# A Fourier convolution with expert routing on one core: the first phase's stores and positions change queues, and its reload comes in three parts

## The chip, the cores and the metric

The kernel runs on one core of one Trainium2 chip. The metric is device time in microseconds (us). Timed runs were made without a profile; one more execution was recorded by the hardware profiler, and every row of a profile below comes from that one.

## The reference

Two computations follow one another. The first is a long causal convolution by Fourier transforms with a filter made by a small network; its product with x is the input of a mixture of experts.

```python
h_mlp = np.maximum(pos_emb @ w1, 0.0) @ w2
h_filt = h_mlp * np.exp(-0.01 * pos)[:, None]
u = x * v                                    # (4, 11456, 128)
y = irfft(rfft(u, n=2S, axis=1) * rfft(h_filt, n=2S, axis=0), n=2S, axis=1)[:, :S]
x = (x * y).reshape(B * S, D)
...
out[do_compute] = xc + gate_w * (relu(xc @ w1[e]) @ w2[e])   # the best expert of each token
```

Rows of the product whose score against w_skip isn't positive are passed through; each other row goes to its best expert of eight. All of it is in float32.

## The kernel before, in words

The transform of length 3840 (three blocks of the sequence) is done in two stages, of 60 and of 64 points. The program has three parts, one after the other: first_phase makes the first stage, freq_phase the second stage, the product with the filter and the first stage back, and out_phase the last stage back, the routing and the experts.

**first_phase** interleaves two generators on the same engines. `First.data(step, pool)` handles one of 16 steps for the first quarter of the features. A step loads a block of x and v of 768 KB (`load`, L178, tile xv), multiplies the two (`mult`, L185), and runs two half steps: each does two matmuls with the 60-point table (L202) into PSUM and two copies by ScalarE into a staging tile (L204). A step's result, 120 rows of 1536 floats, is stored to DRAM as x1d (`store`, L190). All of xv, us (the product) and xs (staging) lie in a tile named wf in the profile; there are 3, 2 and 4 buffers of them. `First.filt` makes the filter's side. It first runs 12 pieces: positions of 256 KB are loaded (`positions`, L232, tile post, 4 buffers, issued 3 pieces ahead), multiplied with w1 (L240) and put through a relu by ScalarE (L241, tile h). Then, for 8 chunks with 3 blocks each, it makes small matmuls with w2 (L267), multiplies by the window on VectorE (L268), does the 60-point stage (L248), and ScalarE copies into fx (L250, 2 buffers each for two halves). After the third block of a chunk the two halves of fx, 120 rows each, are stored as x1f (L256). `first_phase` advances the filter's generator by some two yields for each half step, so that both end together.

Loads run up to three steps ahead (`ahead`). A store of x1d is put off: `data` appends it to a list at the end of its step, and `store` issues it after the first half of the next step, or at once after the last step of a quarter.

**Queues.** Each engine issues its DMAs in its own program order, and a DMA that has to wait holds up what is queued behind it on that engine. Before the change SyncE issues the loads of xv and all stores of x1d, alternating; GpSimd issues the positions and the stores of x1f; ScalarE issues four small loads at the start. In the queue lists of the profile SP is SyncE.

**freq_phase** runs 60 iterations, 15 for each quarter of the features. `load(n)` (L359 to L363) brings the tables c2 (first quarter only), a slice of x1d (128 rows, 4 by 384 floats) and of x1f into the tile x, up to three iterations ahead, in 4 buffers. An iteration does the 64-point stage on TensorE (L373, tile xp), the products with the filter on VectorE (L385, L393), sums on GpSimd (L465, L466), the stage back on TensorE (L404), copies by ScalarE (L405), and a store of z (L414, zd). In the first three quarters it also runs the first stage of the next quarter: `others` calls `mult`, `ahead` and `data` with SyncE's queue for its stores. Six half steps of that (LEAD, three steps) run before the first iteration, on loads that the first phase has issued; the later products run on GpSimd.

The first iteration can only start when its x has landed, which needs x1d of all 16 steps and all of x1f.

Of the kernel before, what the change touches and what calls it, by code (L numbers as in the profile page):

```python
# [22 lines left out]
K1, N2 = 60, 64  # L23
# [5 lines left out]
DH = D // NP  # L29
W = D + 1  # L30
# [113 lines left out]
class First:  # L144
# [3 lines left out]
    Q = 2  # L148
# [3 lines left out]
    XV, US, XS = 3, 2, 4  # L152
# [17 lines left out]
    def ahead(self, step):  # L170

        while self.loaded < min(step + self.XV, self.ALL):
            self.load(self.loaded)
            self.loaded += 1
# [11 lines left out]

    def store(self):

        for dst, xs in self.late:
            self.nc.sync.dma_start(dst, xs)  # L190
        self.late = []

    def data(self, step, pool):
        nc, Q, RUN = self.nc, self.Q, self.RUN
# [3 lines left out]
        for q in range(Q):  # L198
# [6 lines left out]
            if q == 0:  # L205
                self.store()
            if q < Q - 1:
                yield
        self.late.append((self.x1d[h][:, :, 2 * Q * ch:2 * Q * (ch + 1)].rearrange("k c m w -> (k c) m w"), xs))
        if ch == self.STEPS - 1:  # L210
            self.store()
        yield

    def filt(self, fc, fp, pool):


        nc, i = self.nc, self.i
# [11 lines left out]
        def positions(blk, k):  # L229

            pt = fp.tile([128, P], F32, name="post", bufs=4)
            nc.gpsimd.dma_start(pt, i["post"][blk, k // P])  # L232
            return pt
        posts = [positions(*pc) for pc in pieces[:3]]
        yield
        for n, (blk, k) in enumerate(pieces):
            if n + 3 < len(pieces):
                posts.append(positions(*pieces[n + 3]))
            ps = pool.tile([128, P], F32, name="fa")
            nc.tensor.matmul(ps, w1, posts.pop(0), start=True, stop=True)  # L240
            nc.scalar.activation(hs[blk][:, k:k + P], ps, AF.Relu)  # L241
            yield

        def forward(ch, blk, hw, xs):
# [9 lines left out]
            for p in range(2):  # L254
                n0 = p * H2 + ch * M
                nc.gpsimd.dma_start(self.x1f[:, :, n0:n0 + M].rearrange("k c m w -> (k c) (m w)"),  # L256
                                    xs[p].rearrange("k m h s d -> k (m h s d)"))
# [18 lines left out]
def first_phase(tc, fi):  # L276

    with (
# [8 lines left out]
        pace = (pieces - FLEAD) / (fi.Q * (fi.STEPS - FEND))  # L287
        next(f)
# [18 lines left out]
def freq_phase(tc, nc, i, fi, zd, c3, spare, loads):  # L307
# [9 lines left out]
    with (  # L317
# [35 lines left out]
        def load(n):  # L353
# [8 lines left out]
            nc.sync.dma_start(x1[:, :, 0:fi.RUN], fi.x1d[h][ks].rearrange("k c n w -> (c n) k w"))  # L362
            nc.sync.dma_start(x1[:, :, fi.RUN:], fi.x1f[ks, :, :, h * w:(h + 1) * w].rearrange("k c n w -> (c n) k w"))  # L363
            return x1
# [995 lines left out]
```

## Time and profile before

| | us |
|---|---|
| median of 3 runs | 1625.7 (1624.03 to 1628.4) |
| the profiled execution | 1626.78 |
| its span on the core | 1625.0 |
| TensorE (PE) busy | 1537.8 |
| VectorE (DVE) busy | 1203.4 |
| GpSimd (POOL) busy | 1084.8 |
| ScalarE (ACT) busy | 794.3 |
| first L373, where the second stage starts | 142.78 |

The median is 1.1 us below the profiled execution, and the span 1.8 us below it. Times in rows count from the span's start. In rows of the timeline the columns are start, duration, engine, line, operation, tiles and count, and in brackets the idle time before and what ended it; SPq, ACTq and so on are the engines' instruction queues. The list by windows gives for each stretch its length, then busy time and number of instructions of PE, PEld (weight loads), DVE, ACT and POOL, then the granted TensorE clock, the DMA engines' mean busy share and the GB/s moved; the share adds up the time of packets, and can pass 1. A row of waits names who waited, for what, us in total, how often, and the longest.

### The profile page before, as it was taken

How to read it: one execution, taken by the hardware profiler on the slowest of the kernel's cores; microseconds unless marked ns; L12 is line 12 of the kernel's file. 1: busy time of each engine (PE TensorE's matmuls, PEld its weight loads, DVE VectorE, ACT ScalarE, POOL GpSimd, SP SyncE). 2: the span in 40 equal slices, each digit the busy share in tenths (PEclk: the TensorE clock that was granted, in tenths of full speed). 3: DMA queues.
4: the chain of work that ended last, by engine and by line, in shares of the span. 5: the costliest groups of instructions: out<-in, count | busy, mean ns of one | idle time of the engine just before them, and what ended most of it. 6: DMA issues, size and time to landing. Idle time of an engine off the chain costs nothing.

```text
span 1625.0 us, 26505 instructions
## 1 busy us (share of the span) xinstructions
PE 1537.8 (95%) x8272; PEld 961.0 (59%) x8272; DVE 1203.4 (74%) x2424; ACT 794.3 (49%) x1677; POOL 1084.8 (67%) x850
## 2 busy tenths in 40 slices
PE   7985999999999999996789999999989999999997
PEld 2552444444444444442347766666767888888997
DVE  1324877888788799993877777777887777777886
ACT  4552455444544544442235544544345655556774
POOL 1112988888888878870156647855677888867885
PEclk9996999999999999997889999999999999999999
DMA  7998999999999799968978768877631111111110
GB/s 283 333 339 315 379 377 377 356 329 335 321 343 338 255 265 316 312 160 295 301 222 255 229 214 257 255 223 240 209 87 33 47 45 47 45 37 37 38 36 23
DMA packets 198532, 361.92 MB, mean 223 GB/s; under 512 B 64650, under 2 KB 138778, under 8 KB 198350
## 3 DMA queue, kind: packets, MB, share of 16 engines
q1 hardware_dynamic: 181078, 320.12, 58.9%
q0 software_dynamic: 16704, 38.89, 8.5%
q8 instruction: 67, 1.10, 0.3%
q10 hardware_dynamic: 608, 1.20, 0.2%
q14 instruction: 75, 0.61, 0.1%
HBM read 216.96 MB, written 145.69 MB: 223 GB/s over the span
## 4 chain that ended last, share of the span: by engine, by line
PE 84%; DMA 6%; DVE 5%; issue 3%; POOL 1%; ACT 1%; SPq 0%; DVEq 0%; ACTq 0%; POOLq 0%
PE ps L404 20%; PE xp L373 12%; PE bank L782 6%; PE y L1018 5%; PE ps L202 5%; PE my L834 4%; PE my L832 4%; PE hp L700 4%; PE my L833 4%; PE hp L702 4%; PE hp L701 4%; PE mh L700 2%; PE tp L1031 2%; PE mh L702 1%; PE mh L701 1%
## 5 line engine op out<-in xcount | busy, mean ns | idle before, releaser
L404 PE MATMUL ps<-y,c 128*128 128x512 f32 x720 | 331.3, 597 | 0.3
L465 POOL TENSOR_TENSOR y<-y,p 128x2048 f32<-128x2048 f32 x59 | 267.7, 4537 | 68.8 <-DVE p L393 68.8
L706 POOL DMA_INDIRECT out<-o,ids x186 | 199.9, 1075 | 123.3 <-DVE o L713 87.0
L404 PEld LDWEIGHTS ps<-y,c 128*128 128x128 f32 x720 | 133.4, 190 | 173.0 <-issue 155.9
L637 POOL DMA_INDIRECT xt<-out,ids x186 | 193.1, 1038 | 49.3 <-issue 30.6
L393 DVE TENSOR_TENSOR p<-xp,g 128x1024 f32<-128x1024 f32 x240 | 217.4, 947 | 0.0
L393 DVE TENSOR_TENSOR y<-xp,g 128x1536 f32<-128x1536 f32 x120 | 210.8, 1757 | 4.1
L821 DVE SCALAR_TENSOR_TENSOR hh<-hp,hh 128x1024 fp32r<-128x1024 f32 x130 | 158.4, 1219 | 68.3 <-ACT hh L820 68.1
L405 ACT COPY z<-ps 128x512 f32<-128x512 f32 x180 | 105.6, 586 | 176.5 <-PE ps L404 167.5
L820 ACT ACTIVATE hh<-hp 128x1024 fp32r<-128x1024 f32 x130 | 134.2, 1032 | 75.4 <-PE hp L702 75.4
L589 POOL DMA_INDIRECT lists<-pl,lies x32 | 53.6, 1676 | 141.0 <-DVE step L1116 72.3
L466 POOL TENSOR_TENSOR y<-y,p 128x1024 f32<-128x1024 f32 x59 | 139.0, 2356 | 4.6
L677 DVE TENSOR_TENSOR ws<-wf,ws 128x1024 fp32r<-128x1024 f32 x104 | 126.7, 1219 | 15.5 <-ACT ws L672 12.1
L610 POOL MEMSET idle<- 128x512 f16 x248 | 134.6, 543 | 0.2
L1018 PE MATMUL y<-zt,c 128*64 128x512 f32 x384 | 114.1, 653 | 19.8 <-DMA zt<-zd 11.2
L700 PE MATMUL hp<-hl,ws 128*128 128x512 f32 (+1 forms) x344 | 123.3, 359 | 3.5 <-DVE tb L626 1.9
L202 PE MATMUL ps<-wf,c 60*120 60x384 f32 x512 | 111.8, 532 | 14.8 <-DVE wf L185 14.3
L782 PEld LDWEIGHTS bank<-wd,h 128*128 128x128 f32 x896 | 104.2, 191 | 31.5 <-issue 31.4
L373 PE MATMUL xp<-x,wf 128*128 128x480 f32 x256 | 115.5, 575 | 7.3 <-issue 3.6
L204 ACT COPY wf<-ps 120x384 f32<-120x384 f32 x256 | 105.5, 493 | 29.5 <-PE ps L202 28.9
L702 PE MATMUL hp<-hl,ws 128*128 128x512 f32 (+1 forms) x344 | 116.4, 338 | 0.0
L834 PE MATMUL my<-hh,ws 128*128 128x512 f32 (+1 forms) x344 | 116.3, 338 | 0.0
(162 smaller groups left out, 3062.1 us busy)
## 6 DMA issues: line engine op xcount, KB each, us to landing
wf<-xv SPq DMA_DIRECT2D x64, 768.0 KB
zt<-zd SPq DMA_DIRECT2D x64, 768.0 KB
x1d<-wf SPq DMA_DIRECT2D x64, 720.0 KB
x<-x1d SPq DMA_DIRECT2D x60, 768.0 KB
zd<-z SPq DMA_DIRECT2D x118, 384.0 KB
out<-xm SPq DMA_DIRECT2D x96, 258.0 KB
ox<-xo SPq DMA_DIRECT2D x96, 256.0 KB
x1f<-fx POOLq DMA_DIRECT2D x16, 720.0 KB
```

The lines of the kernel that those rows point to most:

```text
L202: nc.tensor.matmul(ps[p], self.c1[rows], u[rows, q * RUN:(q + 1) * RUN], start=True, stop=True)
L373: nc.tensor.matmul(xp[:, k, 0:(NS + NB) * DH], c2(n % PER * KS + j * KH + k), x1[:, j * KH + k], start=True, stop=True)
L393: nc.vector.tensor_tensor(o[:, :, :, j * KH:(j + 1) * KH].rearrange("p s a k b d -> p (s a) k b d"), x[:, None].broadcast_to([128, m, KH, ...
L404: nc.tensor.matmul(zps, c3[:, a, :], y[:, blk, a], start=(a == 0), stop=(a == 1))
L465: nc.gpsimd.tensor_tensor(y[:, 1:], y[:, 1:], p1, ALU.add)
L637: ins = nc.gpsimd.indirect_dma_start(out=xt[:, j], out_offset=None, in_=self.rows[0:have], in_offset=bass.IndirectOffsetOnAxis(ap=ids[:, j ...
L700: nc.tensor.matmul(hp, w[:, 0, c], hl[:, 0], start=True, stop=False)
L702: nc.tensor.matmul(hp, w[:, 1, c], hl[:, 0], start=False, stop=True)
L706: ins = nc.gpsimd.indirect_dma_start(out=self.rows, out_offset=bass.IndirectOffsetOnAxis(ap=ids[:, j:j + 1], axis=0), in_=o, in_offset=Non ...
L782: nc.tensor.matmul(bank[:, j * D:(j + 1) * D], h[f][:, j * 128:(j + 1) * 128], wd[s][:, f * D:(f + 1) * D], start=(f == 0), stop=(f == F / ...
L834: nc.tensor.matmul(y, w2[:, 1, c], h[:, 0], start=False, stop=(f == F // 128 - 1))
L1018: nc.tensor.matmul(y[p * 64:(p + 1) * 64], c4s[ch // C4][:, ch % C4, p, :], z[:, NP * p:NP * (p + 1)], start=True, stop=True)
```

## The change

In the first phase four things are moved, and one in the second:

- Stores of x1d of the first quarter are issued by ScalarE right behind the copies that fill their staging tile, at the end of their own step. Of the 120 rows ScalarE's queue takes 112 (EVEN) and GpSimd's the last 8. Stores of the later quarters stay whole on SyncE's queue, but also at the end of their own step.
- Each store of x1f becomes two, of 112 and 8 rows, both from GpSimd.
- Positions are loaded by SyncE, four pieces ahead and not three: two before the first load of xv, two behind it, and each later one behind the matmul that frees its buffer.
- In the first iteration's reload, x1d comes in two parts around x1f: positions 0 to 47 of the 64 in each half of the rows (steps 0 to 11), then x1f, then the last 16. These are five DMAs in place of two.

The diff, cut to its core:

```diff
@@ -27,6 +27,7 @@
 N = L * NS
 NP = 4
 DH = D // NP
+EVEN = 2 * K1 // 16 * 16
 W = D + 1
 T = 256
 
@@ -167,9 +168,9 @@
         nc.sync.dma_start(self.c1, i["c1"])
         self.loaded, self.late = 0, []
 
-    def ahead(self, step):
-
-        while self.loaded < min(step + self.XV, self.ALL):
+    def ahead(self, step, most=XV):
+
+        while self.loaded < min(step + most, self.ALL):
             self.load(self.loaded)
             self.loaded += 1
 
@@ -184,10 +185,18 @@
             eng = self.nc.vector if step < self.STEPS + LEAD // self.Q else self.nc.gpsimd
             eng.tensor_tensor(self.us[step % self.US][rows], xv[:, 0], xv[:, 1], ALU.mult)
 
+    def shares(self, eng):
+
+        nc = self.nc
+        if eng is nc.sync:
+            return [(slice(0, 2 * K1), eng)]
+        return [(slice(0, EVEN), eng), (slice(EVEN, 2 * K1), nc.gpsimd)]
+
     def store(self):
 
-        for dst, xs in self.late:
-            self.nc.sync.dma_start(dst, xs)
+        for dst, xs, eng in self.late:
+            for rows, by in self.shares(eng):
+                by.dma_start(dst[rows], xs[rows])
         self.late = []
 
     def data(self, step, pool):
@@ -202,13 +211,10 @@
                 nc.tensor.matmul(ps[p], self.c1[rows], u[rows, q * RUN:(q + 1) * RUN], start=True, stop=True)
             for p in range(2):
                 nc.scalar.copy(xs[:, 2 * q + p], ps[p])
-            if q == 0:
-                self.store()
             if q < Q - 1:
                 yield
-        self.late.append((self.x1d[h][:, :, 2 * Q * ch:2 * Q * (ch + 1)].rearrange("k c m w -> (k c) m w"), xs))
-        if ch == self.STEPS - 1:
-            self.store()
+        self.late.append((self.x1d[h][:, :, 2 * Q * ch:2 * Q * (ch + 1)].rearrange("k c m w -> (k c) m w"), xs, nc.sync if h else nc.scalar))
+        self.store()
         yield
 
     def filt(self, fc, fp, pool):
@@ -229,15 +235,17 @@
         def positions(blk, k):
 
             pt = fp.tile([128, P], F32, name="post", bufs=4)
-            nc.gpsimd.dma_start(pt, i["post"][blk, k // P])
+            nc.sync.dma_start(pt, i["post"][blk, k // P])
             return pt
-        posts = [positions(*pc) for pc in pieces[:3]]
+        posts = [positions(*pc) for pc in pieces[:2]]
+        yield
+        posts += [positions(*pc) for pc in pieces[2:4]]
         yield
         for n, (blk, k) in enumerate(pieces):
-            if n + 3 < len(pieces):
-                posts.append(positions(*pieces[n + 3]))
             ps = pool.tile([128, P], F32, name="fa")
             nc.tensor.matmul(ps, w1, posts.pop(0), start=True, stop=True)
+            if n + 4 < len(pieces):
+                posts.append(positions(*pieces[n + 4]))
             nc.scalar.activation(hs[blk][:, k:k + P], ps, AF.Relu)
             yield
 
@@ -253,8 +261,10 @@
                 return
             for p in range(2):
                 n0 = p * H2 + ch * M
-                nc.gpsimd.dma_start(self.x1f[:, :, n0:n0 + M].rearrange("k c m w -> (k c) (m w)"),
-                                    xs[p].rearrange("k m h s d -> k (m h s d)"))
+                there = self.x1f[:, :, n0:n0 + M].rearrange("k c m w -> (k c) (m w)")
+                here = xs[p].rearrange("k m h s d -> k (m h s d)")
+                for rows in (slice(0, EVEN), slice(EVEN, 2 * K1)):
+                    nc.gpsimd.dma_start(there[rows], here[rows])
         last = iter(())
         for ch in range(H2 // M):
             xs = [fp.tile([2 * K1, M, NP, NB, DH], F32, name=f"fx{p}") for p in range(2)]
@@ -285,6 +295,8 @@
         left = 0.0
         pieces = NB * 64 * H2 // 512 + 2 * NB * H2 // 4
         pace = (pieces - FLEAD) / (fi.Q * (fi.STEPS - FEND))
+        next(f)
+        fi.ahead(0, 1)
         next(f)
         fi.ahead(0)
         fi.mult(0)
@@ -359,8 +371,16 @@
                 nc.sync.dma_start(c2(ks.start, KS), i["c2"][k])
             x1 = qx.tile([128, KS, (NS + NB) * DH], F32, name="x1")
             w = NB * DH
-            nc.sync.dma_start(x1[:, :, 0:fi.RUN], fi.x1d[h][ks].rearrange("k c n w -> (c n) k w"))
+            def rows(lo, hi):
+                for c in range(2):
+                    nc.sync.dma_start(x1[c * N2 + lo:c * N2 + hi, :, 0:fi.RUN], fi.x1d[h][ks, c, lo:hi].rearrange("k n w -> n k w"))
+            if n == 0:
+                rows(0, N2 - 16)
+            else:
+                nc.sync.dma_start(x1[:, :, 0:fi.RUN], fi.x1d[h][ks].rearrange("k c n w -> (c n) k w"))
             nc.sync.dma_start(x1[:, :, fi.RUN:], fi.x1f[ks, :, :, h * w:(h + 1) * w].rearrange("k c n w -> (c n) k w"))
+            if n == 0:
+                rows(N2 - 16, N2)
             return x1
 
         def spread(n, j):
```

## The prediction

> **What bounds the kernel now.** I read the chain of waits first, to see which stretches aren't TensorE work. Its answer over the whole span names the longest pieces in order of time; these are the ones around the end of the first phase, and two from behind it.
>
> ```profile
> 17.23 8.31 DMA post<-post
> ...
> 118.83 18.50 DMA x1d<-wf
> 138.06 4.58 DMA x<-x1f
> 142.78 5.36 PE xp L373 x8
> 166.58 3.43 PE ps L404 x8
> 176.68 3.43 PE ps L404 x8
> ```
>
> From 142.78 us on the chain is TensorE, with one piece of L404 every 10.10 us (176.68 - 166.58). Ahead of that stand DMA landings: a block of positions early on, then the last store of x1d, which takes 18.50 us, then the reload. So whatever makes the first xp (L373) start earlier moves all that follows by the same amount, as long as the second stage keeps its 10.10 us. The question is thus what sets 142.78.
>
> Next I asked for engine busy times by window. In each row the last two columns are the DMA engines' mean busy share and the GB/s moved.
>
> ```profile
> 0.00:30.00 30.00, 18.92 (x38) 6.15 (x40) 3.83 (x4) 10.63 (x19) 6.88 (x16) 0.90 0.91 335
> 30.00:45.00 15.00, 15.00 (x120) 8.72 (x118) 4.87 (x7) 8.79 (x19) 0.74 (x2) 0.98 0.60 167
> 45.00:130.00 85.00, 70.78 (x488) 40.85 (x484) 23.73 (x32) 42.49 (x92) 7.61 (x15) 0.92 0.96 339
> 60.00:110.00 50.00, 46.77 (x341) 27.58 (x340) 16.05 (x21) 24.74 (x54) 5.18 (x10) 0.97 0.96 337
> 130.00:142.70 12.70, 5.83 (x16) 2.42 (x16) 1.66 (x2) 3.44 (x8) 0.00 (x0) 0.50 0.59 198
> 160.00:250.00 90.00, 89.92 (x254) 39.19 (x253) 72.58 (x89) 45.17 (x118) 81.54 (x30) 1.00 1.02 378
> ```
>
> The first phase is bound by transfers: from 45 to 130 us the share stands at 0.96, though not at the 1.02 of the second stage. It has a hole at 30 to 45 us (0.60, 167 GB/s) and another after 130 us (0.59, 198 GB/s). The waits of 45 to 130 us agree: engines wait for landings of loads and of stores, and SyncE's queue stands 52.5 us at the x1d stores for ScalarE's copies.
>
> ```profile
> DVE wf L185 <- DMA wf<-xv: 21.9, 6, 8.3
> ACT fx L250 <- DMA x1f<-fx: 11.9, 5, 2.8
> ```
> ```profile
> SPq L190 <- ACT wf L204: 52.5, 11, 8.3
> ```
>
> **Part one: 112 and 8 rows.** The transfers of the phase, from the page's list of issues and the list for 0 to 150 us:
>
> ```profile
> wf<-xv SPq DMA_DIRECT2D x64, 768.0 KB
> x1d<-wf SPq DMA_DIRECT2D x64, 720.0 KB
> ...
> x1f<-fx POOLq DMA_DIRECT2D x16, 720.0 KB
> ```
> ```profile
> post<-post POOLq DMA_DIRECT2D x12, 256.0 KB
> ```
>
> A quarter of the 64 belongs to the first phase: 16 loads of 768 KB against 16 and 16 stores of 720 KB, so 35% of these bytes are loads (128 rows) and 65% stores (120 rows). Suppose a store of 120 rows uses 15 of the 16 DMA engines, 8 rows each. Then each of the 15 carries 0.35/16 + 0.65/15 = 0.0652 of the bytes and the sixteenth 0.0219; if the 15 never rest, the mean share is (15 + 0.0219/0.0652)/16 = 0.958. The rows show 0.96. With 112 rows (7 to each engine) and the last 8 spread over further engines, each carries 0.0625, which is 4.1% less. From 45 us to the last landing (118.83 + 18.50 = 137.33) that is 92 x 0.041 = **3.8 us**. The Trainium skill has the same rule ("DMA: Bandwidth & Descriptors", section "Why a DMA increments its semaphore by 16 and not by 1": a transfer runs on the largest number of engines up to 16 that divides its rows, so 15, 16 and 8 here); no row of this trace shows a transfer of 8 rows.
>
> The bounds: nothing if the sixteenth isn't the reason, and 9.5 us if the stretch then reaches the second stage's 378 GB/s (92 x (1 - 339/378)). I take 3.8, since the share in the row is the one that 15 engines give.
>
> The price is issues. GpSimd gets 16 x 8-row issues and 16 more for x1f, SyncE loses 16 and ScalarE gains 16.
>
> ```profile
> L256 POOL DMA_DIRECT2D x1f<-fx x15 | 7.8, 525 | 62.3 <-ACT fx L250 62.3
> ```
> ```profile
> L190 SPq DMA_DIRECT2D x1d<-wf x21: 348/349/2376, 16.8 to 169.6; - x21
> ```
>
> GpSimd: 32 x 0.525 = 17 us, hidden, as it is idle 62.3 us in that stretch alone. It now stands in order at x1d rows and x1f rows, both released by ScalarE's copies in the order of its queue. ScalarE: 16 x 0.35 = 5.6 us, or 16 x 2.38 = 38 us if each issue is as slow as the slowest. Its room is 50 - 24.74 = 25 us of every 50, so about 50 us in 100: both ends are hidden on average, and I take nothing. Queued behind a slow issue are the copies that free TensorE's accumulators.
>
> **Part two: the opening.** Before, SyncE's queue alternates loads and stores:
>
> ```order
> L178 DMA wf<-xv 128x1536 x4
> L359 DMA wf<-c 128x512
> L190 DMA x1d<-wf 120x1536
> L178 DMA wf<-xv 128x1536
> L190 DMA x1d<-wf 120x1536
> L178 DMA wf<-xv 128x1536
> ```
>
> After the change the same place holds loads and positions (post):
>
> ```order
> L238 DMA post<-post 128x512 x2
> L179 DMA wf<-xv 128x1536
> L238 DMA post<-post 128x512 x2
> L179 DMA wf<-xv 128x1536 x2
> L238 DMA post<-post 128x512 x2
> L179 DMA wf<-xv 128x1536
> L238 DMA post<-post 128x512 x4
> L179 DMA wf<-xv 128x1536
> ```
>
> The first two positions now lead the loads, four are ahead, not three, and no store stands in front of a load. On ScalarE's queue the stores follow the step's own copies:
>
> ```order
> L249 ACTIVATE h_76<-fa 128x512 x2
> L213 COPY wf<-ps 120x384 x2
> L199 DMA x1d<-wf 112x1536
> L249 ACTIVATE h_77<-fa 128x512 x2
> L213 COPY wf<-ps 120x384 x2
> ```
>
> What that does to the hole is read from the timeline of before:
>
> ```profile
> 21.99 0.96 DVE L185 TENSOR_TENSOR wf<-wf 124x768 f32<-124x768 f32 x1 [5.08 <-PE ps L202]
> 25.68 3.75 PE L240 MATMUL fa<-post,fw 128*128 128x512 f32 x4 [3.76 <-DMA post<-post]
> 33.52 2.31 PE L267 MATMUL fa<-fw,h 128*64 128x128 f32 x32
> 34.51 0.35 SPq L190 DMA_DIRECT2D x1d<-wf  x1
> 34.95 0.33 SPq L178 DMA_DIRECT2D wf<-xv  x1
> ```
>
> TensorE stands 3.76 us for a position that took 8.31 us to land; step 2 is late for it, so its store is issued at 34.51, and behind it in the queue a load at 34.95 whose buffer the product of 21.99 freed at 22.95. Meanwhile the DMA engines ran dry. After the change that load waits only for the product, and goes about 12 us earlier. The hole lacks (339 - 167) x 15 us = 2.58 MB against the stretch behind it; at 339/0.96 = 353 GB/s that is 7.3 us. The bounds are nothing and 7.3; I take **6.0**, nearer to the full size, since loads, positions and stores no longer block one another, but the positions now share a queue with loads of 768 KB (2.2 us each at 353).
>
> **Part three: the end of the phase.** Before, the reload of the first x (786 kB from x1d, then x1f) follows all stores. After the change SyncE's queue reads:
>
> ```order
> L179 DMA wf<-xv 128x1536 x10
> L376 DMA x_882<-x1d 48x4x384 x2
> L179 DMA wf<-xv 128x1536 x2
> L381 DMA x_882<-x1f 128x4x96
> L376 DMA x_882<-x1d 16x4x384 x2
> ```
>
> Three quarters of the rows come from steps 0 to 11 and load early; two lead loads stand behind them.
>
> ```profile
> 113.94 3.19 ACT L204 COPY wf<-ps 120x384 f32<-120x384 f32 x8
> 116.84 1.91 SPq L178 DMA_DIRECT2D wf<-xv  x1
> 118.83 1.98 SPq L190 DMA_DIRECT2D x1d<-wf  x1
> 135.61 0.96 DVE L185 TENSOR_TENSOR wf<-wf 124x768 f32<-124x768 f32 x1 [4.90 <-DMA wf<-xv]
> 136.71 2.92 PE L202 MATMUL ps<-wf,c 60*120 60x384 f32 x8 [2.94 <-DVE wf L185]
> ```
>
> The early part is 0.75 x 786 = 590 kB, which costs 590/353 = 1.7 us within the bound stretch. The tail, 137.33 to 142.65 (138.06 + 4.58), is 5.3 us; without those bytes ahead of it, about 4.58 - 1.7 + 1.1 for three issues = 4.0. Net: **-0.4 us** (a loss). The last store is issued at the end of its copies, 117.13, not at 118.83 behind a load: **1.7 us** (from nothing, if the bytes alone count, to 4.4 us, the two lead loads that no longer stand ahead of it). What is late next is the last lead load: from the product at 135.61 to the end of L202 at 139.63 are 4.0 us, as long as the new tail, so TensorE isn't held longer by it.
>
> **Part four: the lead stores and the second stage.** There a store of x1d stays on SyncE, but now follows its own step, not the one before.
>
> ```profile
> 165.06 0.38 SPq L362 DMA_DIRECT2D x<-x1d  x1
> ...
> 181.25 0.42 SPq L190 DMA_DIRECT2D x1d<-wf  x1
> 181.78 1.24 SPq L414 DMA_DIRECT2D zd<-z  x2
> ```
> ```profile
> 182.59 1.63 ACT L204 COPY wf<-ps 120x384 f32<-120x384 f32 x4
> ```
> ```profile
> 190.05 1.77 PE L373 MATMUL xp<-x,wf 128*128 128x480 f32 x4
> ```
>
> The store would wait from 181.25 to 184.22, 3.0 us, with zd and the next loads behind it. Counted from 137.35, the load at 165.06 is the sixth, and its xp starts at 190.05: 25 us between issue and use, against 18.50 for the slowest landing seen. That leaves 6.5 us of cover for 3.0. I take nothing.
>
> **The sum**: 3.8 + 6.0 - 0.4 + 1.7 = 11.1 us. The profiled execution took 1626.78 us, its span 1625.0; so 1615.7 for it, with the first xp at 131.7. The median of the three runs is 1.1 us below the profiled one: 1625.7 - 11.1 = **1614.6**. What a measurement can tell from no change is 0.3%, 4.9 us.
>
> **The rivals.** *The split brings nothing.* The share of 0.96 could be a limit of mixed traffic, and two transfers would do what one did. For it: 339 GB/s could be the memory's pace for stores. Against it: the share itself, and 378 GB/s later. Then 11.1 - 3.8 = 7.3 us: 1618.4. The Trainium skill says so in "DMA: Bandwidth & Descriptors", section "Rules for kernel authors": two transfers to parts of the partitions aren't worth it, and spreading over the engines' queues gives no bandwidth; the row of 0.96 speaks against the first, for 120 rows.
>
> *The opening stays as it is.* Positions queue behind loads in SyncE's one queue, and TensorE waits as at 25.68. The hole moves but stays, and the last store's 1.7 is eaten by the bytes: 3.8 - 0.4 = 3.4 us, 1622.3. For it: 8.31 us for one position, in a queue without loads.
>
> *Slower: SyncE's queue runs dry in the second stage.* There the transfers are at 1.02 share. If the 3.0 us at each x1d store are lost to the DMA engines, the 15 iterations of the first quarter lose 45 us; less 6.5 of cover and 11.1 gained, 27.4 slower: 1653.1. It decides against the change from (6.5 + 11.1)/15 = 1.2 us lost per iteration. Against it: several transfers are in flight there at once, since x1d, zd and the loads are issued within some 3 us, and none is waited for at once.
>
> **How the numbers follow.** The forecast has 0.67, the split without effect 0.14, the unchanged opening 0.13, the dry queue 0.06. The first two are faster by over 4.9 us (0.81), the third is within it (0.13), the last slower (0.06). The low end takes 9.5 in place of 3.8: 1608.9, rounded to 1609. The high end takes in the unchanged opening: 1622.5.
>
> **What would show it.** In the windows: 30 to 45 us at over 0.9 and 330 GB/s; 45 us to the end of the stores at 1.00 and 350 or more; L373 first at about 131.7; pieces of L404 still 10.10 apart; and 1625.0 - 142.78 = 1482.2 us from the first L373 to the end. I am wrong if that last number grows (the dry queue), if the share stays at 0.96 (the split), or if TensorE still waits some 4 us for a position (the opening).

## The result and the profile after

| | before | after |
|---|---|---|
| median of 14 runs each, us | 1628.64 (1623.03 to 1630.37) | 1632.92 (1628.27 to 1637.09) |
| span of the profiled execution | 1625.0 | 1635.1 |
| first xp (L373, after the change L393) | 142.78 | 149.06 |

The ratio is 1.0029, with a 95% interval of 1.0016 to 1.0041: 1628.64 x 0.0029 = some 4.7 us slower, just under 0.3%. The forecast was 11.1 us faster, and the range ended at 1622.5. The profiled execution of after is one of its 14 runs, the longest (1637.09 us), so the two spans are 10.1 us apart, twice as far as the medians.

The windows of after answer to those of before:

```profile
0.00:30.00 30.00, 20.32 (x43) 6.50 (x43) 3.83 (x4) 12.16 (x22) 1.45 (x6) 0.94 0.92 325
30.00:45.00 15.00, 15.00 (x124) 9.06 (x126) 5.19 (x7) 8.13 (x17) 3.23 (x7) 1.00 0.81 274
45.00:130.00 85.00, 72.95 (x477) 42.32 (x474) 22.75 (x30) 40.96 (x86) 20.30 (x39) 0.84 0.90 301
...
75.00:80.00 5.00, 5.00 (x26) 2.79 (x25) 0.69 (x1) 1.45 (x4) 0.00 (x0) 0.56 0.54 186
80.00:85.00 5.00, 5.00 (x46) 3.15 (x44) 1.77 (x3) 3.68 (x8) 2.60 (x5) 1.00 0.49 149
...
130.00:142.70 12.70, 3.59 (x11) 1.26 (x9) 1.70 (x2) 3.35 (x8) 0.52 (x1) 0.66 0.82 285
160.00:250.00 90.00, 89.75 (x252) 38.73 (x251) 73.49 (x91) 45.26 (x119) 81.71 (x30) 0.99 1.01 374
```

In the columns as before, the hole at 30 to 45 us did fill (274 GB/s, 167 before). But from 45 to 130 us the rate is 301 GB/s where it was 339, at a share of 0.90 where it was 0.96. Two things are in that: new holes, as at 75 to 85 us, and less moved per busy time (301/0.90 = 334 against 339/0.96 = 353). From 160 to 250 us next to nothing has changed.

The chain of waits, from 0 to 160 us and on into the second stage:

```profile
53.30 19.09 DMA x1f<-fx
84.20 12.80 DMA x1f<-fx
109.52 11.75 DMA x1f<-fx
126.00 18.37 DMA x1f<-fx
146.01 3.04 DMA wf<-c
149.06 6.18 PE xp L393 x8
...
173.48 3.43 PE ps L424 x8
183.58 3.43 PE ps L424 x8
193.69 3.43 PE ps L424 x8
```

Stores of x1f now stand in the chain four times, where before had them once up to 160 us. The waits of 45 to 130 us say the same of ScalarE, whose wait for a free fx buffer went from 11.9 to 20.2 us (a second profile of before, below, has 16.2), and of GpSimd, which stands at x1d's 8 rows for ScalarE's copies:

```profile
POOL x1d L199 <- ACT wf L213: 51.8, 10, 8.2
ACT fx L258 <- DMA x1f<-fx: 20.2, 5, 5.8
```

L424 is L404 of before: still 10.10 us apart. From the first xp to the end of the span are 1486.0 us, 1482.2 before. Of these 3.8 us more, 0.6 lie between the first xp and the last one, and 3.1 behind the last one, in the last part of the program, which the change doesn't touch; there the unchanged kernel itself took 906.7 us in one profile and 919.9 in another. The 6.3 us at the first xp are the larger part of the difference, and they carry through: from the first to the last xp are 575.4 to 576.1 us in all profiles of this document but one (577.9, with 112 rows stored and 8 left out). The question is which part of the change the 6.3 us come from.

### The profile page after: what moved, and what is told of

Same layout as the page of the kernel before. It is cut to its first block, busy times and chain, and to the rows that moved or that the text cites. A ratio compares the mean times of both kernels' runs of the same rounds, so it can differ in the third digit from the quotient of the medians.

```text
span 1635.1 us, 26493 instructions
## 1 busy us (share of the span) xinstructions
PE 1545.6 (95%) x8272; PEld 964.0 (59%) x8272; DVE 1203.0 (74%) x2424; ACT 795.5 (49%) x1677; POOL 1095.9 (67%) x870
## 4 chain that ended last, share of the span: by engine, by line
PE 83%; DMA 7%; DVE 6%; issue 1%; ACT 1%; POOL 1%; DVEq 0%; SPq 0%; ACTq 0%; POOLq 0%
PE ps L424 19%; PE xp L393 12%; PE bank L802 5%; PE ps L211 5%; PE y L1038 5%; DMA x1f<-fx 4%; PE my L854 4%; PE my L852 4%; PE hp L720 4%; PE my L853 4%; PE hp L722 4%; PE hp L721 4%; PE mh L720 2%; PE tp L1051 2%; PE mh L722 2%; PE mh L721 1%
## 5 line engine op out<-in xcount | busy, mean ns | idle before, releaser
L424 PE MATMUL ps<-y,c 128*128 128x512 f32 x720 | 331.3, 597 | 0.3
L424 PEld LDWEIGHTS ps<-y,c 128*128 128x128 f32 x720 | 133.4, 190 | 173.0 <-issue 155.5
L211 PE MATMUL ps<-wf,c 60*120 60x384 f32 x512 | 114.8, 541 | 11.1 <-DVE wf L186 11.0
L393 PE MATMUL xp<-x,wf 128*128 128x480 f32 x256 | 118.0, 586 | 5.9 <-DMA wf<-c 3.1
```

Source lines behind the costliest of these rows:

```text
L211: nc.tensor.matmul(ps[p], self.c1[rows], u[rows, q * RUN:(q + 1) * RUN], start=True, stop=True)
L393: nc.tensor.matmul(xp[:, k, 0:(NS + NB) * DH], c2(n % PER * KS + j * KH + k), x1[:, j * KH + k], start=True, stop=True)
L424: nc.tensor.matmul(zps, c3[:, a, :], y[:, blk, a], start=(a == 0), stop=(a == 1))
```

## The experiments

After the result two readings stood against each other. By the first, the split is sound and the extra queue and order are at fault: stores of x1f land late, ScalarE and GpSimd stand for them, the DMA engines run dry at 75 to 85 us. By the second, the split itself costs: more transfers (N), the sixteenth DMA engine, which takes time and brings no bytes (E), GpSimd's in-order queue that carries x1d's 8 rows too (G), or pieces of 8 rows whatever their queue (P). The letters are those of the texts on record.

In each experiment the two numbers to follow are the first xp and the row of 45 to 130 us, whose GB/s divided by the share says how much moves per time that the 16 engines are busy: 353 before, 334 after. It is called the rate at full share below; whether a full share would really bring it is a question of the experiments.

### How far one profile can be trusted

The kernel before, unchanged, profiled once more in a later job:

> The kernel before, unchanged: how far the first xp and the stretch from the first L267 to it move between two profiled executions of one program. If 142.78 and 109.3 us come back within 1 us, differences of 3 us and more between kernels are the kernels' own; if they move by 3 us, the single profiles of the partial changes tell nothing and only timed runs do.

Its timeline of TensorE:

```profile
144.88 6.32 PE L373 MATMUL xp<-x,wf 128*128 128x480 f32 x8 [3.38 <-DMA x<-x1f]
```

Its windows:

```profile
45.00:130.00 85.00, 71.19 (x488) 40.91 (x484) 23.38 (x31) 42.48 (x92) 7.81 (x16) 0.94 0.95 338
```

The first xp is 2.1 us later than in the first profile (142.78); the rate at full share is 338/0.95 = 356, against 353. On the chip of this job the phases behind took longer: 1640.7 us for a program that took 1625.0, and 1651.06 for the run of it beside. So for this and the three runs shared with it only the first phase is compared. The changed kernel without the split and without ScalarE's queue, which was profiled twice (below), moved even more, from 139.82 to 144.31. **Single differences of less than some 4.5 us at the first xp tell nothing**; many of the expectations below were written before this was known and ask more of one profile than it can give. The rate at full share is steadier (353 and 356 for before, 345 and 353 for the other), and so are groups of kernels.

### The change without one part

x1d's 112 rows back on SyncE, its 8 rows still on GpSimd:

```diff
-        return [(slice(0, EVEN), eng), (slice(EVEN, 2 * K1), nc.gpsimd)]
+        return [(slice(0, EVEN), nc.sync), (slice(EVEN, 2 * K1), nc.gpsimd)]
```

> The changed kernel, with the 112 rows of each first-quarter x1d store back on SyncE's queue; the 8 rows stay on GpSimd's. Theory Q (a third queue: with loads, x1d and x1f on three queues that take turns on the DMA engines, x1f lands after 17 to 19 us and not 15, ScalarE stands for its fx buffers, and the transfers run dry behind that): x1f lands within 15 us again, the windows between 60 and 110 us show a share of 0.95 or more in place of 0.82, the first xp comes at 140 us or earlier, and the time is 6 to 10 us below the changed kernel, 1623 to 1627. Theory S (the pieces of 112 and 8 rows and their order in GpSimd's queue hold x1f up): nothing of that moves, 1631 to 1635.

Its windows:

```profile
45.00:130.00 85.00, 70.74 (x476) 41.21 (x472) 22.75 (x30) 40.20 (x88) 20.66 (x40) 0.88 0.94 316
```

First xp at 147.03, ratio 1.0036 (1.0013 to 1.0059). The share is back at 0.94, the rate at full share is not: 336. So ScalarE's queue isn't the cause of the lower rate, or not alone.

All stores whole, 120 rows, ScalarE's queue kept:

```diff
-        return [(slice(0, EVEN), eng), (slice(EVEN, 2 * K1), nc.gpsimd)]
+        return [(slice(0, 2 * K1), eng)]
...
-                for rows in (slice(0, EVEN), slice(EVEN, 2 * K1)):
+                for rows in (slice(0, 2 * K1),):
```

> The changed kernel with both x1d (on ScalarE's queue) and x1f stored whole, in 120 rows; GpSimd has no x1d. Theory Q: three queues remain, so the stall of ScalarE and the dry stretches remain, 1631 to 1636. Theory S: the stall goes, the first xp at 140 us or earlier, 1623 to 1627.

Its windows, and then its timeline of TensorE:

```profile
45.00:130.00 85.00, 72.66 (x472) 41.05 (x468) 23.47 (x31) 42.00 (x91) 7.25 (x14) 0.88 0.91 314
```
```profile
142.77 6.47 PE L393 MATMUL xp<-x,wf 128*128 128x480 f32 x8 [6.66 <-DMA wf<-c]
```

314/0.91 = 345: the rate is back, and the first xp is as early as before. The share of 0.91 says that the dry stretches stay, as with the split. The ratio is still 1.0024 (1.0001 to 1.0047), so leaving out the split alone doesn't undo the timed loss. In its profile the rest behind the first xp is the longer part (1632.9 - 142.77 = 1490.1), so the first phase doesn't explain it.

The change with a third fx buffer, so that ScalarE needn't wait for x1f's stores:

```diff
-            xs = [fp.tile([2 * K1, M, NP, NB, DH], F32, name=f"fx{p}") for p in range(2)]
+            xs = [fp.tile([2 * K1, M, NP, NB, DH], F32, name=f"fx{p}", bufs=3) for p in range(2)]
```

> The changed kernel with three buffers of each half of fx in place of two, so that ScalarE's copies wait for a store of x1f that was issued one chunk earlier. Theory Q: x1f still lands after 17 us or more, but ScalarE's waits for it vanish, the share between 60 and 110 us returns to 0.95 or more, the first xp comes at 136 us or earlier, and the time is 8 to 14 us below the changed kernel, 1619 to 1625. Theory S: the order in GpSimd's queue still holds the stores up, and at most half of that is gained, 1627 to 1633.

Its windows, and then its waits from 45 to 130 us:

```profile
45.00:130.00 85.00, 65.68 (x460) 38.10 (x456) 21.72 (x29) 40.49 (x88) 20.01 (x38) 0.87 0.95 314
```
```profile
POOL x1f L267 <- DMA x1f<-fx: 24.6, 8, 6.9
POOL x1d L199 <- DMA x1f<-fx: 14.2, 4, 7.5
```

First xp at 147.20, ratio 1.0019 (0.9990 to 1.0049). Most of the holes went (share 0.95), the rate at full share didn't come back (331). ScalarE's wait for x1f's stores fell from 20.2 to 13.4 us, and GpSimd now stands for them too. The fx buffer was at most a part of the cause. None of the three texts' gains came: the first xp stayed above 140 us in each.

### The split by itself

The kernel before with the split alone: x1d 112 rows on SyncE and 8 on GpSimd, x1f 112 and 8 on GpSimd.

```diff
+PARTS = slice(0, 112), slice(112, 120)
...
-        for dst, xs in self.late:
-            self.nc.sync.dma_start(dst, xs)
+        for dst, xs, parts in self.late:
+            for rows, eng in zip(parts, (self.nc.sync, self.nc.gpsimd)):
+                eng.dma_start(dst[rows], xs[rows])
```

> The kernel before, with the split alone: x1d of the first quarter in 112 rows on SyncE and 8 on GpSimd, x1f in 112 and 8 rows on GpSimd; positions, order and reload as before. Theory B (the prediction's term: fifteen engines carry the stores, and the balance gives 4.1% of the stretch): share 1.00 and 350 GB/s from 45 to 130 us, and 3 to 5 us below before. Theory W (the stores' pace is set elsewhere, so that a busy sixteenth engine only makes each packet longer): share 1.00 at 335 to 342 GB/s, and within 2 us of before.

Its windows:

```profile
45.00:130.00 85.00, 71.22 (x494) 41.21 (x492) 23.63 (x31) 43.08 (x93) 22.69 (x44) 0.92 0.97 326
```

First xp at 147.57; rate at full share 336; ratio 1.0014 (0.9991 to 1.0037), by itself not told from no change. The share is 0.97 and the holes stay away, and yet fewer GB/s than before (339): the engines are busier and move less. That is the sign of the failed term, and it is near what theory W expected, with a rate even lower than W's. The list of queues for 45 to 130 us shows where: number of packets, MB, and the packets' time as a share of 16 engines, for GpSimd's queue (q0) before and with the split alone.

```profile
q0 software_dynamic: 2298, 11.79, 39.0%
```
```profile
q0 software_dynamic: 2783, 11.85, 44.7%
```

The same MB took a seventh more time there. The trace keeps each packet's start, size and duration: a packet of 6144 bytes (one row of a store) took 275 ns on average on this queue before and 311 ns with the split, and on SyncE's queue 277 and 275. The premise of fifteen engines itself holds. From the same times one can count how many packets were in flight at once: from 45 to 130 us it was exactly 15 for 48% of the time and exactly 16 for 33% before, and 17% and 59% with the split. The sixteenth engine was put to work, and no more bytes came of it.

To see the sixteenth engine without the extra transfers, the kernel before got a zero fill of x1d's and x1f's last 15 rows at the start, and then stored either all 120 rows, or rows 0 to 111, or rows 0 to 104. The second leaves out 8 rows of each store of the first phase and the third 15, which stay zero and change the routing, so that the times behind the first phase mean nothing.

```diff
+PARTS = (slice(0, 112),)
...
+        for to in (x1d[0], x1f):
+            nc.scalar.dma_start(to.rearrange("k c n w -> (k c) (n w)")[105:120], i["none"].rearrange("a b w -> (a b w)")[None, :].broadcast_to([15, N2 * self.RUN]))
...
+            for rows in parts:
+                self.nc.sync.dma_start(dst[rows], xs[rows])
```

> The kernel before, and at its start ScalarE's queue fills rows 105 to 119 of the first quarter's x1d and of x1f with zeros (2.9 MB), the rows that the next two kernels never store; here all 120 rows are stored behind that. It is the base line of the next two, read by the first xp: about 143 to 150 us, later than before by up to the 8 us that the fill's bytes take.

> The same with only rows 0 to 111 of each first-quarter x1d and x1f stored, one transfer each: the last 8 rows are left out (they stay zero), so its time behind the first phase says nothing. 7 rows to an engine if sixteen carry them. Theory E (the sixteenth engine is slow at stores, so that a transfer that uses it lands late): first xp no earlier than in the kernel with all 120 rows, or at most 2 us, though 6.7% of the stores' bytes are gone. Theory W (stores have a pace of their own in the memory, whatever the engines): 4 to 6 us earlier. Prediction's theory B (the engine with most rows sets the end): 5 to 8 us earlier.

> The same with only rows 0 to 104 stored, again 7 rows to an engine, on fifteen engines if the number of rows sets it; the last 15 rows are left out. Theory E: clearly earlier than with 112 rows, by 4 us or more, and 6 to 9 us earlier than with 120. Theory W: 8 to 12 us earlier than with 120, in proportion to the bytes, and some 4 to 6 earlier than with 112. Theory B: as with 112 rows, within 2 us.

The windows of the three, in the order 120, 112 and 105 rows, each kernel in a fence of its own. With 120:

```profile
45.00:130.00 85.00, 73.23 (x530) 42.67 (x528) 24.84 (x33) 45.06 (x96) 8.35 (x16) 0.96 0.95 337
```

With 112:

```profile
45.00:130.00 85.00, 74.22 (x528) 43.52 (x526) 25.23 (x34) 45.51 (x98) 8.26 (x16) 0.92 0.94 318
```

With 105:

```profile
45.00:130.00 85.00, 76.54 (x540) 44.94 (x536) 25.84 (x34) 46.85 (x101) 8.63 (x16) 0.91 0.93 317
```

The fill delays the first L267 to 39.80, 37.82 and 39.92; from there to the first xp are 110.0, 109.2 and 105.7 us. If 15 engines with 8 rows each were the limit, 112 rows (7 to each of 16) and 105 rows (7 to each of 15) would both save an eighth of each engine's store bytes: 0.65/8 = 8%, some 7.5 us of 92. They saved 0.8 and 4.3 us, and the rate at full share was 338 and 341, 355 with 120. With 112 rows 16 packets were in flight for 57% of the time, with 105 rows 15 for 42%, which fits sixteen and fifteen engines. Against a scatter of 2 to 4.5 us the first xps are weak evidence, but 112 rows in one transfer, 16 engines and 7% fewer store bytes brought nothing to be seen: the sixteenth engine was not what the phase lacked. Nor is its work by itself what lowers the rate (E): 105 rows, on 15 engines, lowered it as much.

Which of the pieces costs? First each store in two halves of 60 rows on its own queue, in the kernel before:

```diff
+PARTS = slice(0, 60), slice(60, 120)
...
+            for rows in parts:
+                self.nc.sync.dma_start(dst[rows], xs[rows])
```

> The kernel before, with each store of x1d and x1f of the first phase as two stores of 60 rows on its own queue: the same bytes, 32 transfers more, no transfer of 8 rows and none of 112. From the first L267 to the first L393-like xp (L373 in before) it took 109.3 us before and 113.3 with 112 and 8 rows. N (what costs is the number of transfers): 113 to 114 here, first xp at 147 to 148. E (what costs is the sixteenth engine's work, which brings no bytes): 109 to 110, first xp at 143, share 0.96 and some 339 GB/s as before. G (what costs is GpSimd's queue carrying x1d's 8 rows too): 109 to 111, as SyncE's transfers stay on SyncE.

Its windows:

```profile
45.00:130.00 85.00, 70.37 (x464) 40.15 (x462) 22.95 (x30) 40.55 (x88) 14.20 (x28) 0.89 0.95 317
```

The rate falls here too, to 334, though no sixteenth engine is added (15 packets in flight for 46% of the time); the first xp, 144.76, is within what the kernel before itself shows. Then the split alone again, of x1f only:

```diff
-        self.late.append((..., xs, (slice(0, 2 * K1),) if h else PARTS))
+        self.late.append((..., xs, (slice(0, 2 * K1),)))
```

> The kernel before, with x1f alone in 112 and 8 rows, both on GpSimd's queue; x1d whole on SyncE's. N: half of the 32 transfers, so half of the 4.0 us that both splits cost from the first L267 to the first xp: 111.3. G: GpSimd's queue carries nothing of x1d, so 109 to 110 here, and the cost comes back in the run with x1d split alone. If x1f's stores in two are the cost whatever the queue, 113 here.

And of x1d only:

```diff
-                for rows in PARTS:
+                for rows in (slice(0, 2 * K1),):
```

> The kernel before, with x1d alone in 112 rows on SyncE's queue and 8 on GpSimd's; x1f whole. N: 111.3 us from the first L267 to the first xp. G: 113, since GpSimd's in-order queue now stands at x1d's rows ahead of x1f's stores and positions. If x1f's split is the cost, 109 to 110.

The windows with x1f divided:

```profile
45.00:130.00 85.00, 71.20 (x472) 40.55 (x468) 23.13 (x30) 40.33 (x87) 14.78 (x28) 0.86 0.99 316
```

With x1d divided, windows and timeline of TensorE:

```profile
45.00:130.00 85.00, 70.33 (x470) 40.78 (x469) 23.04 (x30) 39.52 (x86) 12.93 (x26) 0.87 0.96 300
```
```profile
153.41 6.01 PE L377 MATMUL xp<-x,wf 128*128 128x480 f32 x8 [2.90 <-DMA x<-x1f]
```

x1f alone: rate 319, first xp 147.74. x1d alone: 313 and 153.41. By rate and first xp, either half costs at least as much as both together (336 and 147.57), so, as far as single profiles can tell, the number of transfers (N) doesn't set the size. The one run with halves doesn't tell whether pieces of 8 rows are worse than pieces of 60.

Last, 112 and 8 rows with each pair on one queue, which takes x1d's 8 rows off GpSimd: x1d alone, then both, then both in the changed kernel with nothing on ScalarE's queue (positions, the stores' place and the reload stay). The edit is shown for the kernel before; in the changed kernel `shares` names SyncE for both parts.

```diff
-            for rows, eng in zip(parts, (self.nc.sync, self.nc.gpsimd)):
-                eng.dma_start(dst[rows], xs[rows])
+            for rows in parts:
+                self.nc.sync.dma_start(dst[rows], xs[rows])
```

> The kernel before, with x1d alone in 112 and 8 rows, both on SyncE's queue; x1f whole on GpSimd's. With the 8 rows on GpSimd's queue the first xp came at 153.41. G (GpSimd's queue standing at x1d's rows ahead of x1f's stores was the cost): 143 to 146 here. N or P (more transfers, or pieces of 8 rows, whatever the queue): 148 to 153.

> The kernel before, with x1d and x1f in 112 and 8 rows, each pair on its own queue (SyncE's, GpSimd's): as many transfers as with 60 and 60 rows (first xp 144.76) and as with the 8 rows of x1d on GpSimd's (147.57). N: 144 to 145. P (pieces of 8 rows cost more than pieces of 60): 147 to 149. G: 144 to 146.

> The changed kernel with nothing on ScalarE's queue, and each store of 112 and 8 rows on one queue: x1d's both on SyncE's, x1f's both on GpSimd's. With x1d's 8 rows on GpSimd's queue the ratio to before was 1.0036 and the first xp at 147.0; with whole stores 0.9997 and 139.8. G (GpSimd's queue, which stands at x1d's rows ahead of x1f's stores, is the cost): ratio 0.999 to 1.001, first xp at 140 to 142. P (the pieces themselves): 1.003 to 1.004, first xp at 145 to 148.

The windows of the three, x1d alone first:

```profile
45.00:130.00 85.00, 69.65 (x462) 39.75 (x464) 23.08 (x30) 39.81 (x85) 7.24 (x14) 0.86 0.97 314
```

Both:

```profile
45.00:130.00 85.00, 70.66 (x462) 39.83 (x458) 22.28 (x30) 40.96 (x88) 14.72 (x28) 0.85 0.97 315
```

Both in the changed kernel:

```profile
45.00:130.00 85.00, 68.65 (x476) 39.69 (x472) 21.97 (x29) 41.13 (x88) 15.78 (x31) 0.91 0.97 320
```

First xp at 146.28, 145.07 and 146.14, rates 324, 325 and 330; the third was timed at 1.0014 (0.9989 to 1.0039). The rate stays low without GpSimd's queue. The five kernels in which GpSimd carries x1d's 8 rows have a mean first xp of 148.9, the four in which it doesn't 146.3; the two sets overlap (147.74 against 147.03), so a share of that queue in the cost is not settled.

### The opening by itself

Positions alone, on SyncE's queue, two ahead of the loads and four in all, in the kernel before:

```diff
-            nc.gpsimd.dma_start(pt, i["post"][blk, k // P])
+            nc.sync.dma_start(pt, i["post"][blk, k // P])
```

> The kernel before, with the positions alone moved: on SyncE's queue, two ahead of the loads and four in all, every store as before. If the opening's gain is the positions' place, the first L267 starts at 28 to 30 us (33.5 before, 28.2 with the stores behind their own step as well) and the first xp at 139 to 141 (142.78 before); the whole is 2 us faster, about ratio 0.998. If it is the stores that stand ahead of loads, L267 stays at 32 to 34 and the first xp at 142 to 143, ratio 1.000.

The other half, each x1d store behind its own step and the reload in three parts, with positions as before (the reload's lines are those of the change):

```diff
-            if q == 0:
-                self.store()
...
+        self.store()
```

> The kernel before, with each x1d store behind its own step's copies and the three-part reload; positions on GpSimd's queue as before, no split, nothing on ScalarE's queue. The same with positions on SyncE's queue had its first L267 at 28.2 and its first xp at 139.82; positions alone had 33.2 and 144.65. If the stores' place opens the hole: L267 at 29 to 31, xp at 139 to 141. If only the two together do: L267 at 33, xp at 142 to 143 less what the end of the phase gains (1 to 2).

The changed kernel with whole stores and x1d on SyncE, that is positions, the stores' place and the reload together, in two jobs on two chips:

```diff
-        self.late.append((..., xs, nc.sync if h else nc.scalar))
+        self.late.append((..., xs, nc.sync))
...
-                for rows in (slice(0, EVEN), slice(EVEN, 2 * K1)):
+                for rows in (slice(0, 2 * K1),):
```

> The changed kernel without its split and without the third queue: x1d whole on SyncE's queue at the end of its own step, x1f whole on GpSimd's; positions on SyncE and the reload in three parts stay. Theory Q (the third queue costs, the split costs, the opening and the reload gain): the first xp at 134 to 139 us, and 4 to 8 us below before. If opening and reload bring nothing by themselves: the first xp at 142 to 144 us, within 2 us of before.

> The changed kernel with whole stores of 120 rows, x1d's on SyncE's queue (positions on SyncE's, each store behind its own step, the reload in three parts stay). Its ratio was 0.9997 (0.9977 to 1.0016) with the first xp at 139.82, 3 us earlier than before. If that gain is real: ratio 0.998 to 0.999 here, first xp at 139 to 141. If it was scatter (two profiles of the kernel before had 142.78 and 144.88): 1.000, first xp at 142 to 144.

The windows with positions alone, and with the stores' place alone:

```profile
30.00:45.00 15.00, 15.00 (x117) 8.60 (x117) 5.19 (x7) 7.86 (x16) 1.09 (x2) 0.92 0.70 215
```
```profile
30.00:45.00 15.00, 15.00 (x122) 8.98 (x120) 5.19 (x7) 9.02 (x19) 1.10 (x2) 1.00 0.65 187
```
The two together: the timeline of TensorE in the first job, then the chain of waits in the second.

```profile
139.82 6.36 PE L393 MATMUL xp<-x,wf 128*128 128x480 f32 x8 [1.36 <-DMA x<-x1d]
```
```profile
121.02 19.65 DMA x1d<-wf
141.14 2.82 DMA x<-x1d
144.31 6.44 PE xp L393 x8
```

And the windows of the second:

```profile
30.00:45.00 15.00, 15.00 (x127) 9.02 (x127) 5.19 (x7) 9.11 (x19) 1.30 (x2) 1.00 0.83 269
45.00:130.00 85.00, 70.39 (x478) 39.75 (x474) 23.61 (x31) 41.60 (x90) 7.25 (x14) 0.86 0.94 332
```

Positions alone: first L267 at 33.16 (33.52 before), first xp at 144.65, ratio 1.0030 (1.0012 to 1.0048). The stores' place: 32.83 and 142.63. Neither half fills the hole (215 and 187 GB/s at 30 to 45 us). Both together filled it in both profiles (301 and 269 GB/s), with first xp at 139.82 and 144.31. But two other profiles warn against reading much into this window. The changed kernel with the split on own queues has both halves too, and its hole stayed; the kernel before with both split on own queues has neither, and its hole was filled:

```profile
30.00:45.00 15.00, 15.00 (x117) 8.64 (x117) 5.18 (x7) 8.02 (x17) 1.28 (x3) 0.91 0.64 207
```
```profile
30.00:45.00 15.00, 15.00 (x138) 9.62 (x136) 5.84 (x9) 8.83 (x19) 2.12 (x4) 1.00 0.89 300
```

The whole kernel with both halves and whole stores on SyncE has ratios of 0.9997 (0.9977 to 1.0016) and 0.9987 (0.9965 to 1.0008). That is the best version found; it is not told from before. The positions' 0.3% has no place in its profile, whose first phase is as long as before's; it stays unexplained.

### All kernels with the same bytes together

| stores of the first phase | kernels | first xp, us | GB/s at full share, 45 to 130 us |
|---|---|---|---|
| whole, 120 rows | before twice; positions; stores' place; both, twice; all whole with ScalarE's queue | 139.82 to 144.88, mean 143.1 | 345 to 356 |
| 60 and 60 | one | 144.76 | 334 |
| 112 and 8 | after; two queues; three fx; split alone; x1f; x1d; and the three with own queues | 145.07 to 153.41, mean 147.7 | 313 to 336 |

(The one with the zero fill is left out, since the fill delays its phase.) The seven profiles with whole stores and the nine with 112 and 8 rows don't overlap in either column, though in the first by only 0.2 us. The means differ by 4.6 us, with a standard error of 1.0 from the scatter within the two groups, whose kernels differ in other parts too. Compared only with whole stores of the same job, on the same chip, the split ones are later in each: by 4.5 us on average of three (142.77 whole), by 5.9 of two (144.65), by 1.9 of two (143.76, two whole) and by 1.8 (144.31), and by 6.3 between before and after. So a cost of the split at the first xp is shown, of some 2 to 6 us. The rate at full share, too, is lower with split stores in each of these jobs.

The timed medians say less. Without the split and without ScalarE's queue the loss is gone (0.9997 and 0.9987; the intervals end at 1.0016 and 1.0008, and after's begins at 1.0016). With one of the two left it isn't settled: 1.0024 with ScalarE's queue alone, 1.0036 and 1.0014 with the split alone in the changed kernel, with intervals that overlap. So how the 4.7 us divide between the two stays open.

## Why the prediction was wrong

**Part one, the split, was the step that failed, and in its sign**: 3.8 us of gain were put down, 4.6 us of loss (some 2 to 6 by jobs) are what the groups show. The steps up to the share were right for the split itself: 16 packets in flight took the place of 15, and the share rose from 0.96 to 0.97 with the split alone. The step from there to time was "each carries 0.0625, which is 4.1% less", which holds only if a packet takes as long as before. It did not: on GpSimd's queue the share went from 39.0% to 44.7% for the same MB. The rates at full share fell instead, from 353 to 336 in the split alone, 5%, which over the 92 us of the term is 4.6 us. The share adds up the time of packets, so longer packets raise it without a byte more. That 0.96 is what 15 engines of 16 give was well observed, but it didn't show that the 15 were the limit. The bound "nothing if the sixteenth isn't the reason" left out the side below nothing, and no reason had been given that excluded it. The rival that the split brings nothing came nearer, and with it the rule of the Trainium skill ("DMA: Bandwidth & Descriptors", "Rules for kernel authors") against two transfers to the two halves of the partitions; the runs agree with it and go further, to a loss. The same table there advises to make one transfer of many small ones, and calls what is below 64 KB mostly overhead. The 8 rows are 48 KB; but the halves of 360 KB, which had no such piece, came out nearer to whole stores in the first xp alone (144.76), not in the rate (334).

**"I take nothing" for ScalarE and GpSimd** held for their issues' own time (most of ScalarE's 16 took 0.31 us, the longest 1.84). What was queued behind them didn't hold: GpSimd waited 51.8 us at x1d's rows and ScalarE 20.2 us for fx, and the DMA engines ran dry at 75 to 85 us. Removing most of these holes alone (three fx buffers, share 0.95) left the first xp at 147.20. Whether the third queue by itself costs anything is open: its first xp is within the scatter with whole stores (142.77), 2 us beyond with split ones (149.06 and 147.03), and its ratio with whole stores is 1.0024 (1.0001 to 1.0047), against 0.9997 and 0.9987 without it.

**Part two, the opening's 6.0 us**: the hole filled to 269 to 327 GB/s in six of the seven kernels with both halves and stayed at 207 in the seventh, while one without them reached 300. Without the split, the first xp of opening and reload together is 142.3 on average of three (139.82, 144.31, 142.77), against 143.8 for the two profiles of before. That is 1.5 us of the 7.3 that parts two and three put down (6.0 - 0.4 + 1.7), and not told from nothing. Two things were weak in the working: the position of 25.68 and the store of 34.51 were read from one execution, and the first xp alone moves by 2 to 4.5 us between executions of one program; and the bytes moved early were counted as time won, though the stretch behind then ran at 328 and 332 GB/s, not at the 339 of before. The rival of an unchanged opening was the better one here, though it, too, came with 3.8 us for the split.

**Part three** held in size. From the last landing to the first xp were 5.45 us (142.78 - 137.33); with the reload in three parts and whole stores 144.31 - 140.67 = 3.64, where 4.0 had been put down. In after it is 4.69 (149.06 - 144.37): there the store that landed last is one of x1f, so the whole x1f part and the last of x1d still had to come. The row puts the end of the wait down to a table, wf<-c, issued at 146.01; by the program that is the second iteration's, the first one's was issued at 23.34, so the last part of x1d, issued from 145.12 on, is the likelier one. That is argued, not shown. The last store's 1.7 us can't be seen under the rest.

**Part four** held: pieces 10.10 us apart, 374 GB/s. The stretch from the first xp to the end, whose growth was to be the sign of a dry queue, did grow by 3.8 us, but only 0.6 of it lie in the second stage (575.5 us from the first to the last xp before, 576.1 after), where the dry queue was priced at 45. The kernel came out slower all the same, by a mechanism that no rival had.

## What to carry to other kernels

A busy share of the DMA engines just under 1 says that they are occupied, not that one more engine would move more: here dividing the stores of a stage at 0.96, to fill the last 4%, made it slower. Try a large store in one piece before dividing it, and ask of each gain that could be nothing whether it could be a loss. Before an opening or a first stage is tuned from one profile, take a second one of the same program: here it moved the very time that was to be won.

## What the runs showed that was not expected

- Dividing stores of 720 KB in two lowers what the DMA engines move at full share: 345 to 356 GB/s whole, 334 in halves, 313 to 336 in 112 and 8 rows. With fewer rows in one transfer, 112 or 105, it is 338 and 341. What in the engines or the memory makes the packets longer, no run here shows.
- Putting the sixteenth DMA engine to work brought no bandwidth: 353 GB/s at full share with 15 packets in flight most often, 336 with 16.
- The first xp of one program moved by 2.1 us (142.78, 144.88) and by 4.5 us (139.82, 144.31) between two profiled executions in different jobs. The second stage didn't scatter: TensorE was busy for 89.92 us of the 90 from 160 to 250 us in all four.
